# Local attention in products of one head each (64 rows by 32 columns), with the values' product placed beside the next tile's scores

## The chip, the cores and the metric

The kernel runs on one core of one Trainium2 chip. The metric is the device time of one execution in microseconds (us); lower is better. Three runs of the kernel before took 1142.04, 1142.9 and 1143.69 us, so the median is 1142.9 us.

## The reference

The program computes an attention over local windows, and two feed-forward stages behind it. All arrays are fp32.

```python
# q, k, v: (4, 8, 768, 64); mem_k, mem_v: (4, 8, 8, 64)
for c in range(nc):                       # chunks of 32 queries
    l_start, r_end = max(0, 32*c - 16), min(S, 32*c + 32 + 8)
    k_full = concat([mem_k, k[:, :, l_start:r_end]])   # up to 64 keys
    scores = scale * q_c @ k_full.T
    a = exp(scores - max); a = a / (sum(a) + 1e-9)
    out[:, :, c_start:c_end] = a @ v_full
x = out as (3072, 512)                    # heads side by side
x = (sigmoid(x @ w_gate) * (x @ w_val)) @ w_out        # 512 -> 1536 -> 512
x = silu(x @ w_in) ; x = x @ w_out2                    # 512 -> 2048 -> 512
```

## The kernel before, in words

Tokens are cut into 24 tiles of 128 (`NTILE`), and four tiles make a block of 512 (`BLOCKS1`). A tile has 4 chunks of 32 queries and 8 heads, so 32 pairs of chunk and head, each with 32 queries against 64 keys.

**Attention of one tile.** It has four parts that the program places one by one.
- Scores (`att_scores`): 16 fp32 products. Each takes two heads at once: the queries lie in a tile with zeros beside them (`qh` has 16x2x32 columns, half of them zero), so that 128 rows by 64 columns of weights hold two heads of 64 dimensions with 32 queries each. 64 keys stream through. Two such products stand side by side in TensorE's columns (`scv[cp*64 : ...]`). The profile's tile is `sc`, line L195. VectorE then takes the maximum and subtracts it (L208, L209), ScalarE takes the exponential (L210, tile `e`).
- Normalising (`att_norm`): four VectorE operations, L216 to L219.
- Turning (`att_turn`): four 128x128 transposes on TensorE (L225, tile `pt`), copied out by ScalarE (L226, tile `at`).
- Values' product (`att_pv`): 16 fp32 products with 32 columns of weights and 128 streaming columns (two heads side by side, `vb` has zeros for the other head), four side by side (L235, tile `px`); VectorE places the result in `x32` with a block transpose (L242).

**Stages.** In the opening stage the four tiles of the first block are done one after the other, with spare transposes of the identity (`idle`, tile `warm`, L389) between their parts; the queries, keys and values come by DMA from SP's queue, and the first three weights of the gated stage behind them. Then come six blocks of the gated stage. In each, `f` runs over 12 slices: a gate product `pg` and a value product `pv` (12 matmuls each, L269), their sigmoid and product on ScalarE and VectorE, and one slice late the output product `y` (12 matmuls, L89 to L93). Each slice has three steps: after `pg` (step 0), after `pv` (step 1) and after `y` (step 2). A hand-written table (`events`) puts the parts of the next block's four attention tiles at steps: scores at step 3, 11, 19 and 27 of a block's 36, normalising 2 later, turning 4 later, the values' product 6 later. Beside the first block the weights are split into high and low parts (`Feed`), beside the others the second stage's weights are prepared (`prepare2`). At the last slice of a block `split_x` makes the next block's `x` from `x32`: four ScalarE casts (L81), four VectorE subtractions (L84). After the sixth block follows the second stage (`pair2`, `out2`), which has no attention in it.

PSUM has eight banks: two `m` (`pg`, `pv`), four `y` (in the opening stage also `sc` and `px`), two `att` (`sc`, `pt`, `px` of the loop).

Of the kernel before, what the change touches and what calls it, by code (L numbers as in the profile page):

```python
# [15 lines left out]
P = 128  # L16
# [19 lines left out]
NQ = ()  # L36
# [10 lines left out]
def moe_kernel(ctx: ExitStack, tc: tile.TileContext, qh, kh, vh, wg, wv, wo, w2i, w2o, out):  # L47
# [6 lines left out]
    ps = ctx.enter_context(tc.tile_pool(name="ps", bufs=1, space=PSUM))  # L54

# [16 lines left out]
    def ps_y(name):  # L72
        return ps.tile([P, 512], F32, tag="y", name=name, bufs=4)

    def ps_a(name):
        return ps.tile([P, 512], F32, tag="att", name=name, bufs=2)
# [90 lines left out]
    def att_load_qk(t, qb, kt):  # L167
        nc.sync.dma_start(out=qb.rearrange("p g u q -> p (g u q)"), in_=qh[t])
        nc.sync.dma_start(out=kt.rearrange("p a c k -> p (a c k)"), in_=kh[t])
        q_t[t], k_t[t] = qb, kt  # L170

    def att_load_v(t, vb):
        n = 4 // len(vb) * 256
        for h, v in enumerate(vb):
            for u in range(2):
                nc.sync.dma_start(
                    out=v[u * 64 : u * 64 + 64, u].rearrange("p c j d -> p (c j d)"),
                    in_=vh[t, u * 64 : u * 64 + 64, h * n : h * n + n],
                )
        v_t[t] = vb  # L180

    def zero_v(vb, eng):
        for v in vb:
            for u in range(2):
                eng.memset(v[u * 64 : u * 64 + 64, 1 - u], 0.0)

    def att_scores(t, ps_sc, e):
        sc = ps_sc(f"sc{t}")
        scv = sc.rearrange("p (c2 a k) -> p c2 a k", c2=2, a=4)
# [12 lines left out]
        if t % TPB == 0:  # L202
            nc.vector.memset(scv[0:64, 0, :, NMEM : NMEM + LEFT], NEG)
        if t % TPB == TPB - 1:
            nc.vector.memset(scv[64:128, 1, :, WIN - RIGHT : WIN], NEG)
        s3 = sc.rearrange("p (g k) -> p g k", k=WIN)
        m = att.tile([P, 8, 1], F32, tag="m", name=f"m{t}", bufs=2)
        nc.vector.tensor_reduce(m, s3, axis=AX.X, op=ALU.max)  # L208
        nc.vector.tensor_tensor(out=e, in0=s3, in1=m.to_broadcast([P, 8, WIN]), op=ALU.subtract)  # L209
        nc.scalar.activation(out=e, in_=e, func=AF.Exp, scale=SCALE)  # L210
        e_t[t] = e

    def att_norm(t, eng=nc.vector):
        e = e_t[t]
# [4 lines left out]
        eng.tensor_tensor(out=e, in0=e, in1=r.to_broadcast([P, 8, WIN]), op=ALU.mult)  # L219

    def att_turn(t, ps_pt, at):
        e = e_t.pop(t).rearrange("p g k -> p (g k)")
        pt = ps_pt(f"pt{t}")
        for i in range(4):
            nc.tensor.transpose(pt[:, i * P : (i + 1) * P], e[:, i * P : (i + 1) * P], ident)  # L225
        nc.scalar.copy(at.rearrange("p a b q -> p (a b q)"), pt)  # L226
        at_t[t] = at

    def att_pv(t, ps_px, xt, off):
# [726 lines left out]
```

## Time and profile before

| | |
|---|---|
| median of 3 runs | 1142.9 us |
| the profiled execution | 1142.29 us |
| its span | 1140.3 us |
| TensorE (PE) busy | 1128.1 us, 99% |
| VectorE (DVE) busy | 640.3 us, 56% |
| ScalarE (ACT) busy | 486.8 us, 43% |
| granted TensorE clock | 1.00 of full speed, in all 40 slices |

PE's rows are matmuls; PEld's are their weight loads, which overlap them. A row's duration is that of one instruction from its start to its modelled end; matmuls overlap, so the distance between starts, and the pieces of the chain of waits, tell what a matmul costs in a stream. A matmul on plain fp32 is recorded as two rows: 16 products of `sc` are 32 rows. DMA queues are written as SPq.

### The profile page before, as it was taken

The numbers are of one execution on the slowest core, as the hardware profiler recorded it, in microseconds if no ns is written. First come the engines' busy times: TensorE is split into PE (matmuls) and PEld (weight loads), VectorE is DVE, ScalarE is ACT, GpSimd is POOL, SyncE is SP. The second block draws the span as 40 slices with busy tenths as digits, with TensorE's granted clock in tenths as the row PEclk, the third lists the DMA queues.
The fourth block names the chain that finished last, engine by engine and source line by source line (L and its number), as shares of the span: only waits on it lengthen the run. The fifth ranks groups of instructions, "written<-read, shape, count | busy, mean of one in ns | idle before, by whom it ended". The sixth has DMA issues, their size and how long they took to land.

```text
span 1140.3 us, 15875 instructions
## 1 busy us (share of the span) xinstructions
PE 1128.1 (99%) x6319; PEld 924.6 (81%) x6319; DVE 640.3 (56%) x947; ACT 486.8 (43%) x708; POOL 49.4 (4%) x44
## 2 busy tenths in 40 slices
PE   7999999999999999999999999999999999999998
PEld 6788888888888887888878888888888888888887
DVE  7887744555454545554454433448843479543665
ACT  2766533343344424443332324444534445344442
POOL 1000000000000000000000001101011110011000
PEclk9999999999999999999999999999999999999999
DMA  9898766667675766676573446575665566655552
GB/s 312 308 301 281 283 220 207 230 198 228 219 230 186 222 215 213 213 235 209 175 245 142 147 158 230 193 282 198 228 214 194 213 258 223 228 191 205 189 214 79
DMA packets 79209, 248.50 MB, mean 218 GB/s; under 512 B 7584, under 2 KB 23968, under 8 KB 69920
## 3 DMA queue, kind: packets, MB, share of 16 engines
q1 hardware_dynamic: 79136, 247.49, 63.7%
q8 instruction: 50, 0.82, 0.3%
q14 instruction: 23, 0.19, 0.0%
HBM read 199.23 MB, written 48.23 MB: 217 GB/s over the span
## 4 chain that ended last, share of the span: by engine, by line
PE 95%; DMA 4%; DVE 1%; SPq 0%; ACT 0%; issue 0%; DVEq 0%; ACTq 0%
PE o L786 20%; PE c L673 20%; PE pv L269 17%; PE pg L269 16%; PE y L89 6%; PE y L91 6%; PE y L93 6%; PE sc L195 2%; PE px L235 2%; DMA vA<-in_vh_dram 1%; DMA stg_wo<-in_wo_dram 1%; PE pt L225 1%; DMA stg_wg<-in_wg_dram 1%; DMA yd<-y 1%; DMA w2i_d<-coi 0%; DMA k<-in_kh_dram 0%
## 5 line engine op out<-in xcount | busy, mean ns | idle before, releaser
L673 PE MATMUL c<-xp,wr 128*128 128x512 f32 x1008 | 229.1, 389 | 0.0
L786 PE MATMUL o<-gf,wr 128*128 128x512 f32 x1008 | 229.0, 389 | 0.0
L673 PEld LDWEIGHTS c<-xp,wr 128*128 128x128 f32 x1008 | 189.2, 188 | 39.3
L786 PEld LDWEIGHTS o<-gf,wr 128*128 128x128 f32 x1008 | 189.2, 188 | 39.3
L269 PE MATMUL pg<-x,w 128*128 128x512 f32 x864 | 209.9, 392 | 2.0 <-ACT x L81 2.0
L269 PE MATMUL pv<-x,w 128*128 128x512 f32 x864 | 210.9, 393 | 0.2 <-DVE sg L284 0.2
L269 PEld LDWEIGHTS pg<-x,w 128*128 128x128 f32 x864 | 160.6, 188 | 37.1 <-ACT x L81 2.9
L269 PEld LDWEIGHTS pv<-x,w 128*128 128x128 f32 x864 | 160.2, 188 | 35.6 <-issue 2.4
L84 DVE TENSOR_TENSOR gf<-g,gf 128x1024 fp32r<-128x1024 f32 x84 | 103.8, 1239 | 49.9 <-ACT gf L81 49.6
L81 ACT CAST gf<-g 128x1024 fp32r<-128x1024 f32 x84 | 88.1, 1053 | 86.8 <-PE o L786 71.5
L286 ACT CAST g<-sg 128x512 fp32r<-128x512 f32 x72 | 44.7, 621 | 136.3 <-DVE sg L284 136.3
L279 ACT ACTIVATE sg<-pg 128x512 f32<-128x512 f32 x72 | 42.9, 596 | 93.4 <-PE pg L269 79.5
L693 POOL TENSOR_TENSOR s<-s,s 128x512 f32<-128x512 f32 x24 | 36.0, 1498 | 956.2 <-ACT s L692 956.2
L289 DVE TENSOR_TENSOR g<-sg,g 128x512 fp32r<-128x512 f32 x72 | 49.8, 691 | 42.5 <-ACT g L286 42.5
L645 DVE TENSOR_TENSOR s<-c,s 128x512 f32<-128x512 f32 x48 | 33.2, 691 | 65.1 <-PE c L673 63.1
L89 PE MATMUL y<-g,wor 128*128 128x512 f32 x240 | 66.2, 397 | 0.7 <-DVE y L547 0.7
L284 DVE TENSOR_TENSOR sg<-pv,sg 128x512 f32<-128x512 f32 x72 | 49.3, 685 | 29.6 <-PE pv L269 29.6
L91 PE MATMUL y<-g,wor 128*128 128x512 f32 x240 | 64.3, 390 | 0.0
L93 PE MATMUL y<-g,wor 128*128 128x512 f32 x240 | 64.1, 389 | 0.0
L648 DVE TENSOR_TENSOR g<-g,g 128x1024 f32<-128x1024 f32 x48 | 58.4, 1216 | 0.0
L651 ACT ACTIVATE g<-s 128x512 f32<-128x512 f32 x48 | 30.3, 632 | 54.1 <-DVE s L645 54.1
L91 PEld LDWEIGHTS y<-g,wor 128*128 128x128 f32 x240 | 45.1, 188 | 9.6
(113 smaller groups left out, 987.5 us busy)
## 6 DMA issues: line engine op xcount, KB each, us to landing
wr<-w2o_d SPq DMA_DIRECT2D x42, 1024.0 KB, 4.8
wor<-wo_d SPq DMA_DIRECT2D x60, 512.0 KB, 4.8
wr<-w2i_d SPq DMA_DIRECT2D x24, 1024.0 KB, 5.1
wr<-w2i_d SPq DMA_DIRECT2D x24, 768.0 KB, 4.4
w2o_d<-coo SPq DMA_DIRECT2D x56, 256.0 KB, 2.9
w2i_d<-coi SPq DMA_DIRECT2D x24, 512.0 KB, 3.0
qA<-in_qh_dram SPq DMA_DIRECT2D x21, 512.0 KB, 5.0
k<-in_kh_dram SPq DMA_DIRECT2D x21, 512.0 KB, 5.7
```

What stands on the lines that cost most here:

```text
L81: nc.scalar.copy(hi, src)
L84: lo_eng.tensor_tensor(out=lo, in0=src, in1=hi.bitcast(F32), op=ALU.subtract)
L89: nc.tensor.matmul(o, w_hi, x_hi, start=first, stop=False)
L91: nc.tensor.matmul(o, w_hi, x_lo, start=False, stop=False)
L93: nc.tensor.matmul(o, w_lo, x_hi, start=False, stop=last)
L269: nc.tensor.matmul(o[:, :n], w[:, pw, kt * P : (kt + 1) * P], x[kt][:, px, :n], start=i == 0, stop=i == len(steps) - 1,)
L284: nc.vector.tensor_tensor(out=sg[:, :n], in0=psv[:, :n], in1=sg[:, :n], op=ALU.mult)
L286: nc.scalar.copy(g[:, 0, :n], sg[:, :n])
L289: nc.vector.tensor_tensor(out=g[:, 1, :n], in0=sg[:, :n], in1=g[:, 0, :n].bitcast(F32), op=ALU.subtract)
L648: nc.vector.tensor_tensor(out=o, in0=a, in1=b_, op=ALU.subtract)
L673: nc.tensor.matmul(o, w[:, pw, i % 4, kt * P : (kt + 1) * P], X[i][:, px, kt], start=first and j == 0, stop=j == 5, skip_group_check=not f ...
L786: nc.tensor.matmul(c[at[i], dp], w[:, pw, pl, dp * P : (dp + 1) * P], f[:, px, pl], start=i in (A11, S1, S2) and pp == 0 and j == 0, stop= ...
```

## The change

- The data come without zeros and without doubled keys: `qh` has 512 columns instead of 1024, `kh` 768 instead of 1024 (two neighbouring chunks share one stretch of 96 keys), and the values' tile 1024 instead of 2048. The clearing of the values' tiles (`zero_v`) goes. Each tile has three loads (queries, keys, values).
- Scores: 32 products instead of 16, each of one head and chunk: 64 rows by 32 columns of weights, 64 keys streaming. Consecutive products take the eight places of a grid of two row halves (`u`) and four column quarters (`c`). The two row halves write to two PSUM banks.
- Values' product: 32 products instead of 16, on the same grid, with 64 streaming columns instead of 128.
- In the loop the values' product of a tile and the next tile's scores stand together ("meet"), in one PSUM tile of two banks, and the tiles of a block begin 9 steps apart, the first four at 3, 11, 18 and 26. Normalising comes 4 steps after the scores, turning 6 after.
- In the opening stage the multiplication of three of the four tiles goes from VectorE (one 128x512 operation) to ScalarE (eight of 128x64).
- PSUM: `att` is one tile of two banks instead of two tiles of one; in the opening stage `sc` and `px` take turns in two tiles of two banks; the second stage opens its own two banks.

On TensorE in the loop the rows below are from the first block (`px_973` and `sc_1042` are the sixth tile's values' product and the seventh tile's scores; `pg`, `pv`, `y` are the gated stage's matmuls). Before, at its place between `y` and `pg`, and between `pv` and `y`:

```order
L93 MATMUL y_3_605<-g_4_881,wo_895 128x512
L235 MATMUL px_973<-vA,at_921 32x128 x16
L269 MATMUL pg_6_1004<-x_0_445,w_928 128x512 x2
...
L269 MATMUL pv_6_1028<-x_3_454,w_928 128x512
L195 MATMUL sc_1042<-k_816,qA 64x64 x16
L89 MATMUL y_0_602<-g_5_959,wo_993 128x512
```

Now, at one of its places, between `y` and `pg`:

```order
L96 MATMUL y_2_755<-g_7_1367,wo_1381 128x512
L96 MATMUL y_3_756<-g_7_1367,wo_1381 128x512
L243 MATMUL sx_1459<-v_1215,at_1408 32x2x32 x32
L189 MATMUL sx_1459<-k_1251,q_1250 32x64 x32
L281 MATMUL pg_9_1547<-x_0_579,w_1414 128x512 x2
```

Two insertions of 16 products in the stream of large matmuls have become one of 64 smaller ones.

On VectorE at the end of the first block (`px_1462` and `sx_1709` hold the last tile of the second block; `x_0` to `x_3` are the low parts of the new `x`; `sg_11` is the gated product that frees `pv`'s bank). Before:

```order
L289 TENSOR_TENSOR g_10_1423<-sg_10_1387,g_10_1423 128x512
L242 STREAM_TRANSPOSE x_1_727<-px_1462 128x4x4x32
L130 TENSOR_TENSOR wo_1482<-t_wo_1441,wo_1482 128x512
L84 TENSOR_TENSOR x_0_1499<-x_1_727,x_0_1499 128x512
L84 TENSOR_TENSOR x_1_1502<-x_1_727,x_1_1502 128x512
L84 TENSOR_TENSOR x_2_1505<-x_1_727,x_2_1505 128x512
L84 TENSOR_TENSOR x_3_1508<-x_1_727,x_3_1508 128x512
L284 TENSOR_TENSOR sg_11_1460<-pv_11_1486,sg_11_1460 128x512
```

Now:

```order
L301 TENSOR_TENSOR g_10_1663<-sg_10_1629,g_10_1663 128x512
L252 STREAM_TRANSPOSE x_1_924<-sx_1709 128x4x128
L204 TENSOR_REDUCE m_1782<-sx_1709 128x8
L205 TENSOR_TENSOR e_1744<-sx_1709,m_1782 128x2x4x64
L133 TENSOR_TENSOR wo_1786<-t_wo_1688,wo_1786 128x512
L87 TENSOR_TENSOR x_0_1803<-x_1_924,x_0_1803 128x512
L87 TENSOR_TENSOR x_1_1806<-x_1_924,x_1_1806 128x512
L87 TENSOR_TENSOR x_2_1809<-x_1_924,x_2_1809 128x512
L87 TENSOR_TENSOR x_3_1812<-x_1_924,x_3_1812 128x512
L296 TENSOR_TENSOR sg_11_1707<-pv_11_1790,sg_11_1707 128x512
```

The maximum and the subtraction of the next tile's scores now stand between the placing of the values and the new `x`.

On ScalarE in the opening stage (`e` are the exponentials, `at` the copies of the turned tiles, `stg_wg` the first weights). Before:

```order
L210 ACTIVATE e_84<-e_84 128x512
L210 ACTIVATE e_w<-e_w 128x512 x2
L226 COPY at_260<-pt_261 128x512
L210 ACTIVATE e_w<-e_w 128x512
L226 COPY at_307<-pt_308 128x512
L226 COPY at_351<-pt_352 128x512
L107 ACTIVATE stg_wg_132<-stg_wg_132 128x512
L226 COPY at_387<-pt_388 128x512
```

Now:

```order
L211 ACTIVATE e_w<-e_w 128x512
L223 ACTIVATE e_90<-e_90,r_236 128x64 x8
L211 ACTIVATE e_w<-e_w 128x512
L231 COPY at_296<-pt_297 128x512
L223 ACTIVATE e_w<-e_w,r_310 128x64 x8
L211 ACTIVATE e_w<-e_w 128x512
L231 COPY at_366<-pt_367 128x512
L223 ACTIVATE e_w<-e_w,r_380 128x64 x8
L231 COPY at_433<-pt_434 128x512
L110 ACTIVATE stg_wg_114<-stg_wg_114 128x512
L231 COPY at_485<-pt_486 128x512
```

Three groups of eight small multiplications have come in between the exponentials and the copies.

The core of the diff:

```diff
     def att_load_v(t, vb):
-        n = 4 // len(vb) * 256
-        for h, v in enumerate(vb):
-            for u in range(2):
-                nc.sync.dma_start(
...
+        nc.sync.dma_start(out=vb, in_=vh[t])
         v_t[t] = vb
-    def att_scores(t, ps_sc, e):
...
+    def att_scores(t, sx, e):
+
+        sc = sx[:, :, :256].rearrange("p u (a k) -> p u a k", a=4)
         qb, kt = q_t.pop(t), k_t.pop(t)
-        for c2 in range(2):
-            for a in range(4):
-                for cp in range(2):
-                    c = 2 * c2 + cp
+        kv = kt.rearrange("p (a c k) -> p a c k", a=4, c=2)
+        for a in range(4):
+            for c in range(4):
+                for u in range(2):
+                    r = slice(u * 64, u * 64 + 64)
+                    g = (4 * a + c) * CH
                     nc.tensor.matmul(
-                        scv[cp * 64 : cp * 64 + 64, c2, a],
-                        qb[:, 4 * a + c].rearrange("p u q -> p (u q)"),
-                        kt[:, a, c],
+                        sc[c * CH : c * CH + CH, u, a],
+                        qb[r, g : g + CH],
+                        kv[r, a, c // 2, c % 2 * CH : c % 2 * CH + WIN],
                         start=True,
                         stop=True,
                     )
...
     def att_norm(t, eng=nc.vector):
...
+        if eng is nc.scalar:
+            for g in range(8):
+                nc.scalar.activation(out=e[:, g], in_=e[:, g], func=AF.Copy, scale=r[:, g])
+        else:
+            eng.tensor_tensor(out=e, in0=e, in1=r.to_broadcast([P, 8, WIN]), op=ALU.mult)
...
+    def att_pv(t, px, xt, off):
+
         at, vb = at_t.pop(t), v_t.pop(t)
-        px = ps_px(f"px{t}")
         for c in range(4):
-            for j in range(4):
-                q0 = 64 * (c % 2) + 32 * (j % 2)
-                nc.tensor.matmul(
-                    px[32 * j : 32 * j + 32, c * P : (c + 1) * P],
-                    at[:, c // 2, j // 2, q0 : q0 + 32],
-                    vb[c * len(vb) // 4][:, :, c % (4 // len(vb)), j],
...
+            for a in range(4):
+                for u in range(2):
+                    r = slice(u * 64, u * 64 + 64)
+                    g = a * P + c * CH
+                    o = px[a * CH : a * CH + CH, u].rearrange("p (h x) -> p h x", h=2)
+                    nc.tensor.matmul(
+                        o[:, :, c * CH : c * CH + CH],
+                        at[r, g : g + CH],
+                        vb[r, (4 * c + a) * D : (4 * c + a + 1) * D],
...
+        for t in range(n0, NTILE + 1):
+            at = 9 * (t - n0) - 3 if t >= 2 * n0 else (3, 11, 18, 26)[t - n0]
+            events.setdefault(at, []).append(("meet", t))
+            if t < NTILE:
+                events.setdefault(at + 4, []).append(("norm", t))
+                events.setdefault(at + 6, []).append(("turn", t))
...
+                if what == "meet":
+                    sx = ps_att(f"sx{t}")
+                    steps = []
+                    if t > n0:
...
+                        steps.append(att_pv(t - 1, sx[:, :, 256:], x32[bn], jj * P))
+                        prefetch_v(t)
+                    if t < NTILE:
+                        steps.append(att_scores(t, sx, e_tile(t)))
+                        prefetch(t + 1)
+                    for step in steps:
+                        step()
```

The functions' last lines (the softmax in `soften`, the placing in `place`) are now handed back and run after both products have been issued.

## Rows read from the trace of the kernel before

**Rows 1.** The page: busy us of each engine (share of the span) x instructions.
```profile
PE 1128.1 (99%) x6319; PEld 924.6 (81%) x6319; DVE 640.3 (56%) x947; ACT 486.8 (43%) x708; POOL 49.4 (4%) x44
```

**Rows 2.** By stage: busy PE, PEld, DVE, ACT, POOL; PE clock, DMA share, GB/s.
```profile
0.00:29.10 29.10, 22.04 (x351) 19.16 (x351) 21.32 (x41) 8.49 (x14) 4.81 (x14) 1.00 0.93 315
29.10:150.00 120.90, 120.68 (x775) 97.25 (x776) 96.49 (x173) 76.72 (x125) 0.00 (x0) 1.00 0.84 288
150.00:571.90 421.90, 421.52 (x2707) 342.11 (x2709) 209.76 (x387) 166.75 (x253) 0.00 (x0) 1.00 0.65 212
```

**Rows 3.** Chain of waits in order of time, first block: start, duration, what.
```profile
128.02 2.72 PE pg L269 x12
130.74 1.01 PE px L235 x32
131.75 2.94 PE pv L269 x12
...
145.58 2.72 PE pg L269 x12
148.29 1.08 PE sc L195 x32
149.38 2.95 PE pv L269 x12
```

**Rows 4.** TensorE's timeline at 191.1 and 197.8 us, each once short, once whole.
```profile
191.10 0.32 PE L235 MATMUL px<-vA,at 128*32 128x128 f32 x4
...
191.10 1.08 PE L235 MATMUL px<-vA,at 128*32 128x128 f32 x32
...
197.77 0.28 PE L195 MATMUL sc<-k,qA 128*64 128x64 f32 x2
...
197.77 1.15 PE L195 MATMUL sc<-k,qA 128*64 128x64 f32 x32
```

**Rows 5.** Tiles sc and px: durations in ns (least/median/most), first and last start.
```profile
L195 PE MATMUL sc<-k,qA x672: 222/222/270, 5.7 to 554.0; 128*64 128x64 f32 x168
...
L235 PE MATMUL px<-vA,at x672: 272/273/297, 17.9 to 572.0; 128*32 128x128 f32 x168
```

**Rows 6.** Timeline of the opening stage: start, us, what [idle before, releaser].
```profile
1.37 4.14 PE L389 MATMUL warm<-ident 128*128 128x128 f32 x22 [1.37 <-POOL ident masks.py:199]
...
5.69 1.15 PE L195 MATMUL sc<-k,qA 128*64 128x64 f32 x32 [0.18 <-DMA k<-in_kh_dram]
...
23.62 0.69 ACT L107 ACTIVATE stg_wg<-stg_wg 128x512 f32<-128x512 f32 x1 [2.62 <-DMA stg_wg<-in_wg_dram]
...
24.20 0.58 ACT L226 COPY at<-pt 128x512 f32<-128x512 f32 x1
...
29.10 3.22 PE L269 MATMUL pg<-x,w 128*128 128x512 f32 x12 [2.02 <-ACT x L81]
```

**Rows 7.** Groups of the opening stage: busy us, mean ns, idle before.
```profile
L226 ACT COPY at<-pt 128x512 f32<-128x512 f32 x4 | 2.3, 575 | 1.9 <-PE pt L225 1.9
L209 DVE TENSOR_TENSOR e_w<-sc,m 128x512 f32<-128x512 f32 x3 | 2.1, 692 | 0.1
L219 DVE TENSOR_TENSOR e_w<-e_w,r 128x512 f32<-128x512 f32 x3 | 2.1, 691 | 0.1
L216 DVE TENSOR_REDUCE r<-e_w 128x8 f32<-128x512 f32 x3 | 2.0, 665 | 0.0
...
L210 ACT ACTIVATE e_w<-e_w 128x512 f32<-128x512 f32 x3 | 1.9, 631 | 6.5 <-DVE e_w L209 6.5
```

**Rows 8.** Timeline at 235.8 to 247.2 us, the end of a block.
```profile
235.76 0.41 ACT L81 CAST coi<-fi 128x256 fp32r<-128x256 f32 x1
...
240.65 1.08 PE L235 MATMUL px<-vA,at 128*32 128x128 f32 x32
...
245.94 0.68 DVE L284 TENSOR_TENSOR sg<-pv,sg 128x512 f32<-128x512 f32 x1
...
247.23 2.88 PE L269 MATMUL pg<-x,w 128*128 128x512 f32 x12
```

More of the change, by code (lines that the diff above doesn't have):

```diff
@@ L35 @@
 LV = 1
-NQ = ()
 NJ = 8
@@ L201, in att_scores, with soften @@
                     )
[L202 to L210, printed above, removed]
-        e_t[t] = e
+        e_t[t] = e
+        def soften():
+            if t % TPB == 0:
+                nc.vector.memset(sc[0:CH, :, :, 0:LEFT], NEG)
+            if t % TPB == TPB - 1:
+                nc.vector.memset(sc[3 * CH : 4 * CH, :, :, WIN - RIGHT : WIN], NEG)
+            m = att.tile([P, 2, 4, 1], F32, tag="m", name=f"m{t}", bufs=2)
+            nc.vector.tensor_reduce(m, sc, axis=AX.X, op=ALU.max)
+            nc.vector.tensor_tensor(
+                out=e.rearrange("p (a u k) -> p u a k", a=4, u=2),
+                in0=sc,
+                in1=m.to_broadcast([P, 2, 4, WIN]),
+                op=ALU.subtract,
+            )
+            nc.scalar.activation(out=e, in_=e, func=AF.Exp, scale=SCALE)
+        return soften
     def att_norm(t, eng=nc.vector):
-        e = e_t[t]
+        e = e_t[t].rearrange("p (g k) -> p g k", g=8)
         r = att.tile([P, 8, 1], F32, tag="r", name=f"r{t}", bufs=2)
@@ L227, in att_turn, with place @@
+    def att_turn(t, pt, at):
+        e = e_t.pop(t)
+        for a in range(4):
+            nc.tensor.transpose(pt[:, a * P : (a + 1) * P], e[:, a * P : (a + 1) * P], ident)
+        nc.scalar.copy(at, pt)
         at_t[t] = at
-    def att_pv(t, ps_px, xt, off):
+    def att_pv(t, px, xt, off):
         at, vb = at_t.pop(t), v_t.pop(t)
-        px = ps_px(f"px{t}")
         for c in range(4):
-            for j in range(4):
-                q0 = 64 * (c % 2) + 32 * (j % 2)
-                nc.tensor.matmul(
-                    px[32 * j : 32 * j + 32, c * P : (c + 1) * P],
-                    at[:, c // 2, j // 2, q0 : q0 + 32],
-                    vb[c * len(vb) // 4][:, :, c % (4 // len(vb)), j],
-                    start=True,
-                    stop=True,
-                )
-        nc.vector.transpose(
-            out=xt[:, :, off : off + P].rearrange("p k (c q) -> p c k q", c=4),
-            in_=px.rearrange("p (c k q) -> p c k q", c=4, k=4),
-        )
+            for a in range(4):
+                for u in range(2):
[6 more added lines that the diff above has]
+                        vb[r, (4 * c + a) * D : (4 * c + a + 1) * D],
+                        start=True,
+                        stop=True,
+                    )
+        def place():
+            nc.vector.transpose(
+                out=xt[:, :, off : off + P].rearrange("p (u h) x -> p u h x", u=2),
+                in_=px.rearrange("p u (h x) -> p u h x", h=2),
+            )
+        return place
@@ L315, in at_tile, with v_tile @@
+        def v_tile(t):
+            return att.tile([P, 16 * D], F32, tag="v", name=f"v{t}", bufs=1)
         def at_tile(t):
-            return att.tile([P, 2, 2, P], F32, tag="at", name=f"at{t}", bufs=1)
+            return att.tile([P, 512], F32, tag="at", name=f"at{t}", bufs=1)
         def e_tile(t):
-            return att.tile([P, 8, WIN], F32, tag="e", name=f"e{t}", bufs=1)
+            return att.tile([P, 512], F32, tag="e", name=f"e{t}", bufs=1)
         def flat(i, name):
             w = w_slot(i, name).bitcast(F32)
-            return [w[:, h].rearrange("p a b -> p (a b)") for h in range(2)]
@@ L340, in moe_kernel @@
-        for t in range(n0):
-            if t == 0:
-                make_identity(nc, ident)
-            zero_v(vs[t], nc.gpsimd if t % 2 else nc.vector)
+            kv = flat(4 + t, f"kv{t}")
+            vs.append(kv[:, :1024])
+            ks.append(kv[:, 1024 : 1024 + 8 * (WIN + CH)])
+            qs.append(qq[:, (t - 1) * 512 : t * 512])
+            es.append(eq[:, (t - 1) * 512 : t * 512])
+        make_identity(nc, ident)
         wo_d = dram.tile([NF1, P, 2, 512], F32, tag="wo_d", name="wo_d")
```

136 lines of the change are left out of this document (58 added, 78 removed).

## The prediction, made before the changed kernel ran

> **What bounds the kernel now.** I read the page first: TensorE is busy 1128.1 of 1140.3 us, the other engines at most 56% [rows 1]. An average can hide stages, so the table by stage came next. The opening stage, up to the first gated matmul at 29.10 us, is the only one in which TensorE has gaps: 22.04 of 29.10 us busy, with the DMA engines at 0.93. In the first block it is busy 120.68 of 120.90 us, in the other five 421.52 of 421.90 [rows 2]. So from 29.1 us on every microsecond of TensorE's time that the attention takes stands in the result, and waits on other engines cost nothing there now. Third, the chain of waits gives the price of attention in that stream: twelve large matmuls take 2.72 us, a scores piece 1.08 and the twelve behind it 2.95, so scores cost 1.08 + 0.23 = 1.31 us; a values piece costs 1.01 + 0.22 = 1.23 us [rows 3]. Together 2.54 us a tile, 50.8 us for the loop's 20 tiles. Last, I opened the timeline around one of each, to see what these pieces are made of.
>
> **What a small product costs.** Thirty-two rows of scores, of 0.222 us each, fill 1.15 us: their starts are spread over 0.93 us. Two stand side by side, and the second starts about 7 ns behind the first (0.28 us for two, 0.270 for the longest one) [rows 4, 5]. So there are 16 pairs in 15 steps of (0.93 - 0.007)/15 = 0.0615 us. The values' 32 rows, 0.272 us each, are spread over 1.08 - 0.27 = 0.81 us; four start within 0.32 - 0.297 = 0.023 us, which makes 8 groups in 7 steps of (0.81 - 0.02)/7 = 0.113 us [rows 4, 5]. The step follows the streaming columns (64 against 128) and not how many products stand side by side: two and four run at the same speed each. Taking 16 x 0.0615 from 1.31 and 8 x 0.113 from 1.23 leaves 0.33 us in both cases: the frame of one insertion, which is the change into small products and back.
>
> **The loop after the change.** A tile now has 32 scores products and 32 values' products, 64 rows each, all with 64 streaming columns. Eight side by side make 8 + 8 groups. If the step stays at 0.0615 us, these take 0.98 us. Eight starts need 7 x 0.007 = 0.05 us, which fits inside a step; at the end the spread adds 0.03 to the frame, 0.36 us, paid once instead of twice. A meeting then costs 1.34 us against 2.54. There are 19 whole meetings, one with scores alone and one with values alone (0.49 + 0.36 = 0.85 us each): 19 x 1.34 + 2 x 0.85 = 27.2 us against 50.8. The gain is 23.5 us. In general, with s for the average distance between small rows, the loop changes by 2560 s - 43.2 us (2560 rows, 21 frames of 0.36, less 50.8). That s is the unknown: no row of before has eight side by side, or products in two row halves. The near end is 0.0615/8 = 7.7 ns. The far end is the distance the values' rows keep today, 0.113/4 = 28.3 ns, which would add 29.2 us. Below the near end lies only the 7 ns of neighbouring starts, 1.8 us better still. I take 7.7 ns, because the step was the same for two and for four, and the starts of neighbours are close enough for eight.
>
> Here a rule of the Trainium skill speaks against the change. The rows give 7 ns between neighbours of one group, yet on average no row follows another by less than 28.3 ns [rows 4]. Its page "TensorE: Matmul & The Clock Gate", section "Wait — 56ns, not 53.3ns?", says that the distance from matmul to matmul never falls under about 25 ns however few columns stream. Read as an average over the whole engine this gives 2560 x 0.025 - 43.2 = 21 us more in the loop, an estimate from that page, and about 1161 us in all. Part 3 of the same page, on packing small matmuls, gives about 4 ns for each further place of the grid; the 7 ns agree with this one, so I read the 25 ns as a bound for one place.
>
> **The rest of the loop.** The transposes, the softmax operations and their durations stay. At the end of a block, VectorE has maximum and subtraction (689 and 692 ns by today's scores, so 1.4 us) between the placing of the values and the new x, and ScalarE has the exponential, 0.63 us, ahead of the casts [rows 7]. In the block end that I looked at, values start at 240.65, the product that frees the value bank starts at 245.94, the new block's gate at 247.23 and its value product 2.72 us later, at 249.95 [rows 3, 8]. Freed at 246.6 now, the bank comes 3.3 us early; about 2.1 us of added work leaves 1.2. The new x is nearer: its last low part ends when L284 starts, 1.3 us before the gate, though only the first of the four is needed at once and the others 0.68 us apart each. I price the four block ends that carry scores at 0.2 us each, 0.8 in all, between 0 and 4 x 2.1 = 8.4. In the first block VectorE is at 96.49 of 120.90 us [rows 2]; losing some 6 us of TensorE's time there raises this to 84%, still no bound. DMAs only get smaller, and SP waits for fewer of them.
>
> **The opening stage.** Before, the last copy of a turned tile (24.20) sits behind the first weights' operation, which waited for its DMA until 23.62; from that copy to the first gate at 29.10 pass 4.9 us [rows 6]. The first eight loads shrink from 8 x 512 KB to 4 x (256 + 384) KB, 1.6 MB less, at 315 GB/s 5.0 us [rows 2]: those weights would land near 18.6 us, and they are no longer last. The engines' own chain is. The first scores can't start before the 22 spare transposes end at 5.51, and before they started at 5.69 [rows 6]: nearly nothing is gained there. VectorE loses three multiplications of 691 ns, and ScalarE gets three groups of eight [rows 7]. One of these eight has 64 columns; a cast of 256 columns takes 0.41 us [rows 8], an operation of 512 takes 0.63 [rows 7], so by a straight line 0.25 us, 2.0 for eight (between 0.63, as one operation, and 8 x 0.41 = 3.3). ScalarE then needs 2.0 + 0.63 + 0.58 = 3.2 us a tile. The first group starts when two tiles have been through maximum and subtraction (1.4 us each) and one through its row sum and what follows it (1.1), so near 5.5 + 0.7 + 2.8 + 1.1 = 10.1 us; three times 3.2 ends the third tile near 19.7; the fourth is normalised on VectorE beside it and turned, and its copy starts some 1.1 us later, near 20.8. With the same 4.9 us behind it the first gate comes at 25.7, 3.4 us earlier. The ends: 5.0 earlier (bytes alone), and 0.5 later (3 x 1.3 us more for the eights).
>
> **The sum**, against the profiled execution's own 1142.29 us (0.6 under the median of 1142.9): 1142.3 - 23.5 - 3.4 + 0.8 = 1116.2. I predict 1116 us.
>
> **Rivals.**
> - *Only four places run at once* (0.12): the two row halves take turns, as if the columns' quarters alone counted. For it: no row before uses half of the rows. Against: nothing in the rows ties a start to its neighbour. s = 0.0615/4 = 15.4 ns, the loop changes by -3.8 us, the opening by about -3: 1142.3 - 6.8 + 0.8 = 1136 us. The change would then not do what it says; only the smaller frame pays.
> - *The supply of small rows is the limit* (0.13), and the kernel gets slower: twice as many rows and weight loads come in an unbroken run of 128 rows, four times as long as any today. For it: no stretch of the trace has rows closer than 28.3 ns on average. Against: that distance is explained by the streaming columns to a few ns, in both shapes. At 28.3 ns the loop is 29.2 us longer and the opening still some 2 us shorter: about 1170 us. The change turns into a loss where 2560 s - 43.2 - 3.4 + 0.8 passes zero, at s = 17.9 ns.
> - *The products are as fast as forecast, but waits take the place of what was saved* (0.07): the block ends at their full price (7.6 us more than I count), or the opening's longer gaps, near 3 us against 2.02 today, lower TensorE's clock to the 1.2 GHz level for the first gate and value products, 24 x 0.227 = 5.4 us. The rows show 1.00 throughout [rows 2], so I give this little. One alone gives 1122 or 1124 us, both 1129.
>
> **How the numbers follow.** The forecast has 0.68, with 1110 to 1124 as its own range: the near bound of s and a full 5.0 in the opening on one side, block ends at half price on the other. The range that should hold 8 in 10 goes on from there to the half-speed rival and a little over it: 1108 to 1140. It leaves out the supply rival and some of the rest. A change of 0.2%, 2.3 us, is about what a measurement of this kernel can tell from none. Faster by more takes in the forecast, the first rival and most of the third: 0.85. Slower by more is the supply rival, 0.12 of its 0.13; the same 0.03.
>
> **What would show each step.** In the timeline of a meeting: 64 rows of values and 64 of scores, the last start about 1.0 us behind the first; eight starts within 0.06 us, then a pause. If the starts come evenly every 15 or 25 ns, one of the first two rivals holds. In the chain: one piece of scores and values together of some 1.1 us, the twelve matmuls behind it 0.2 longer than 2.72. TensorE's idle time after the first gate stays under 2 us in total, otherwise the third rival has its part. The first gate starts between 24 and 27 us, and eight small multiplications take near 2.0 us. The prediction is wrong if a meeting costs more than 1.8 us in the chain, or if the gates at block ends wait for x.

## The result and the profile after

The changed kernel takes 1126.57 us (median of 4 runs, 1125.71 to 1127.12) against 1142.88 us beside it: a ratio of 0.9857, 95% interval 0.984 to 0.9874. It is 16.3 us faster. The forecast was 26 us faster: the sign and the wide range held, the likeliest case's own range (1110 to 1124) did not. Two terms of the sum were mis-sized: the distance of small products in a long piece, and the opening stage, in which TensorE ran out of instructions.

The page's line of busy times, and that of the queue that brings TensorE's instructions (packets, MB, share of the DMA engines). Before, the queue had moved 50 packets, 0.82 MB, for 12,638 matmuls and weight loads; now it is 62 for 15,710, some 253 a packet both times:

```profile
PE 1112.1 (99%) x7855; PEld 917.8 (82%) x7855; DVE 635.0 (56%) x938; ACT 490.8 (44%) x732; POOL 45.3 (4%) x36
...
q8 instruction: 62, 1.02, 0.4%
```

The same three stages as in [rows 2], with the same columns:

```profile
0.00:29.10 29.10, 21.85 (x607) 18.85 (x607) 15.51 (x31) 13.73 (x36) 0.70 (x6) 0.94 0.79 295
29.10:150.00 120.90, 120.06 (x1073) 98.21 (x1074) 99.20 (x179) 78.95 (x128) 0.00 (x0) 0.99 0.76 269
150.00:571.90 421.90, 421.90 (x3760) 347.39 (x3760) 215.69 (x395) 170.26 (x262) 0.00 (x0) 1.00 0.61 205
```

From 150 to 571.9 us TensorE has no gap at all, and the list of its waits has none at the block end before that: the block ends cost nothing. The opening stage has the same busy time in far more instructions, less DMA, and a granted clock of 0.94 where it was 1.00.

The chain of waits through a meeting, and through scores alone (start, us, what; counts are a little low where records are missing), beside [rows 3]:

```profile
40.20 0.79 PE sx L189 x53
40.99 2.99 PE pv L281 x12
...
63.48 0.79 PE sx L243 x53
64.27 0.65 PE sx L189 x42
64.92 2.94 PE pg L281 x12
```

A meeting costs 0.79 + 0.65 + (2.94 - 2.72) = 1.66 us, against 2.54 before and 1.34 forecast; scores alone cost 0.79 + 0.27 = 1.06. TensorE's timeline of the same meeting, its first part cut out once (start, us, what):

```profile
63.42 0.45 PE L243 MATMUL sx<-v,at 64*32 64x64 f32 x32
...
63.42 0.86 PE L243 MATMUL sx<-v,at 64*32 64x64 f32 x64
64.08 0.85 PE L189 MATMUL sx<-k,q 64*32 64x64 f32 x64
64.85 3.01 PE L281 MATMUL pg<-x,w 128*128 128x512 f32 x12
```

One row lasts 0.216 us. The first 32 rows start within 0.45 - 0.216, some 0.24 us, 7.7 ns apart: the eight places do work together, at the forecast distance. But 64 rows start within 0.64 us and all 128 within 64.08 + 0.85 - 0.22 - 63.42 = 1.29 us. The 96 rows behind the first 32 are (1.29 - 0.24)/96 = 11 ns apart; over the whole meeting it is 10.2.

The opening stage, answering to [rows 6] (TensorE, then ScalarE, then TensorE):

```profile
5.30 0.86 PE L189 MATMUL sc<-k,q 64*32 64x64 f32 x64
...
9.29 0.79 PE L189 MATMUL sc<-kv,q_w 64*32 64x64 f32 x57
13.64 0.31 PE L189 MATMUL sc<-kv,q_w 64*32 64x64 f32 x7 [3.56 <-issue]
...
11.03 2.02 ACT L223 ACTIVATE e<-e,r 128x64 f32<-128x64 f32 x8 [0.47 <-DVE r L220]
...
24.89 0.59 ACT L231 COPY at<-pt 128x512 f32<-128x512 f32 x1 [0.26 <-PE pt L230]
...
29.94 4.48 PE L281 MATMUL pg<-x,w 128*128 128x512 f32 x12 [1.96 <-ACT x L84]
```

After 57 of the 64 rows of the third scores tile TensorE stands for 3.56 us, in the middle of one tile's products, and the profile names no releaser. The last copy comes at 24.89 us, not at the forecast 20.8, and the first gate at 29.94, 0.84 us later than before. Its twelve matmuls then take 4.48 us where they took 3.22. Not all of them are slow: the first seven start 234 to 335 ns apart as before, and from about the eighth on, into the value product behind them, the distance is 427 ns, which is the 1.2 GHz level. By stretches (columns as in [rows 2], granted clock third from the end) the clock fell twice: once behind the 3.56 us of idle time, and once 1.6 us into the first gate:

```profile
14.60:17.80 3.20, 3.20 (x46) 2.87 (x45) 1.76 (x5) 2.34 (x8) 0.00 (x0) 0.50 1.04 416
31.60:34.90 3.30, 3.30 (x9) 2.62 (x9) 3.09 (x7) 1.96 (x4) 0.00 (x0) 0.50 0.16 31
```

What the second fall cost is the time from the first gate to the second one, before and after:

```profile
34.90 2.99 PE L269 MATMUL pg<-x,w 128*128 128x512 f32 x12
...
37.32 0.39 PE L281 MATMUL pg<-x,w 128*128 128x512 f32 x1
```

That is 34.90 - 29.10 = 5.80 us and 37.32 - 29.94 = 7.38 us, 1.58 us more.

### The profile page after: what moved, and what is told of

It is laid out like the page before. It is cut to its first block, busy times and chain, and to the rows that moved or that the text cites. A ratio compares the mean times of both kernels' runs of the same rounds, so it can differ in the third digit from the quotient of the medians.

```text
span 1125.3 us, 18936 instructions
## 1 busy us (share of the span) xinstructions
PE 1112.1 (99%) x7855; PEld 917.8 (82%) x7855; DVE 635.0 (56%) x938; ACT 490.8 (44%) x732; POOL 45.3 (4%) x36
## 4 chain that ended last, share of the span: by engine, by line
PE 96%; DMA 2%; DVE 0%; SPq 0%; ACT 0%; issue 0%; DVEq 0%
PE o L808 20%; PE c L695 20%; PE pv L281 18%; PE pg L281 17%; PE y L94 6%; PE y L92 6%; PE y L96 6%; PE sx L243 1%; PE sx L189 1%; DMA k<-in_kh_dram 1%; PE pt L230 1%; DMA kv<-in_vh_dram 1%; DMA yd<-y 1%; SPq L172 0%; SPq L171 0%; DVE x L252 0%
```

## Experiments on the loop

The theory: TensorE's instructions are fed at a limited pace. The first 32 rows of a piece stand ready and run at the forecast 7.7 ns; what follows is fed more slowly. The rival: the eight places themselves are full.

**Half of the columns** (m1). The kept half of the keys and of the values' columns is computed in the loop, the rest set to zero.

```
-   kv[r, a, c // 2, c % 2 * CH : c % 2 * CH + WIN]
+   kv[r, a, c // 2, c % 2 * CH : c % 2 * CH + 32]       # same in values: 32 of 64 columns
+   nc.vector.memset(sc[:, :, :, 32:], 0.0)              # and the other half of the values
```

> The changed kernel with half of the streaming columns left out in the loop: each small product has 32 columns instead of 64 (half of the keys, half of the values' columns; the halves that are left out are set to zero by VectorE). Theory, supply: after its first 32 rows a meeting is fed at 16.7 ns a product (8.3 ns a row) and has pauses of its own; a product half as long changes nothing in that: meetings keep 1.2 to 1.3 us between first and last start, and the time stays within 4 us of the changed kernel's 1126.6 (1122 to 1127). Rival, the eight places are full: with half the columns the distance halves, a meeting's starts spread over some 0.7 us, and the loop is 11 to 13 us shorter: 1114 to 1116.

1126.65 us (ratio 0.9859, 0.9844 to 0.9874). TensorE's timeline of a meeting, its first 32 rows cut out once:

```profile
61.48 0.35 PE L245 MATMUL sx<-v,at 64*32 64x32 f32 x32
...
61.48 0.76 PE L245 MATMUL sx<-v,at 64*32 64x32 f32 x64
62.09 0.75 PE L189 MATMUL sx<-k,q 64*32 64x32 f32 x64
62.77 2.56 PE L286 MATMUL pg<-x,w 128*128 128x512 f32 x10
```

From the first row to the next large matmul pass 1.29 us, against 1.43 in the changed kernel: half of the streaming saves a tenth. Of the values' 64 rows the first 32 start within 0.16 us instead of 0.24, while the 32 behind them take 0.40 us in both kernels. So behind the first 32 rows the eight places are not what is full; something that does not depend on the streaming columns is, and I call it the feed. This run leaves the number and the size of the weight loads as they were, so it does not tell instructions that come slowly from weight loads that go slowly. Against the second stands that 33 weight loads start within 0.20 us at the head of a piece; a run that separates the two was not made. The total did not even fall by 20 x 0.14 = 2.8 us, though the first gate runs at the 2.4 GHz level here (3.19 us): VectorE has the memsets in addition, TensorE waits 1.7 us once for VectorE's product of a gate and a value, and some 2 us stay unexplained.

**Half by half** (m2). The order of the loops alone.

```
-   for a in range(4): for c in range(4): for u in range(2):
+   for u in range(2): for a in range(4): for c in range(4):
```

> The changed kernel with another order of the same products: all of one row half (heads 0 to 63 of the partitions) before all of the other, in scores and in values, so that neighbours in the order use four places and not eight. Theory, TensorE takes instructions in order with at most some 32 rows queued: only four places work at a time, a row each 61.5/4 = 15.4 ns, a meeting of 128 rows costs 2.0 + 0.2 us instead of 1.66, and the loop is some 10 us longer: 1135 to 1139. Rival, supply alone sets the distance of 10 ns, whatever the places: the time stays at 1126 to 1128.

1132.27 us (ratio 0.9903, 0.9887 to 0.992), 5.7 more than the changed kernel, between the two expectations. The timeline of a meeting, its first 0.27 us cut out, and the chain of another:

```profile
63.50 0.47 PE L243 MATMUL sx<-v,at 64*32 64x64 f32 x18
...
63.50 0.99 PE L243 MATMUL sx<-v,at 64*32 64x64 f32 x64
64.30 0.98 PE L189 MATMUL sx<-k,q 64*32 64x64 f32 x64
```

```profile
109.26 0.92 PE sx L243 x61
110.19 0.79 PE sx L189 x60
110.97 2.99 PE pg L281 x12
```

In the 0.27 us in which the changed kernel starts 32 rows, 18 start here, 15 ns apart as four places allow. Rows 33 to 64 of a piece then take 0.40 us, as in the changed kernel, so the loss is smaller than I expected: 1.98 us a meeting against 1.66, about 6 us over the loop. Eight places in turn in the order of the program are worth that much; this part of the forecast's mechanism is shown.

**Apart** (m3). Scores one step ahead of the values instead of behind them in one piece.

```
-   events.setdefault(at, []).append(("meet", t))
+   events.setdefault(at - 1, []).append(("scores", t))
+   events.setdefault(at, []).append(("values", t))
```

> The changed kernel with scores and values at separate places in the loop, one step of some 3 us apart, instead of in one piece: the new products without the meeting. By the chain of the changed kernel scores alone cost 0.79 + 0.27 = 1.06 us and a meeting 1.66. Theory, a frame of 0.36 to 0.4 us is paid once for each insertion, and rows cost 10.2 ns in a piece of 64 as in one of 128: 2.12 us a tile, 19 x 0.46 = 8.7 us more, 1134 to 1137. Rival, the long unbroken run of 128 rows is what makes rows dear (10.2 ns where the first 32 take 8.3): pieces of 64 come cheaper, 1.5 to 1.8 us for the two, and the time is at 1124 to 1130.

1135.55 us (ratio 0.994, 0.9923 to 0.9957). The chain:

```profile
156.34 0.79 PE sx L189 x53
157.13 2.94 PE pg L281 x12
160.07 0.79 PE sx L243 x53
160.86 2.94 PE pv L281 x12
```

Twice 0.79 + 0.22 = 2.02 us against 1.66: the meeting saves one frame of 0.36 us, 19 x 0.36 = 6.8 us. The other 2 of the 9.0 us are waits that this order adds (scores for the copy of a turned tile 1.3 us, values for VectorE 0.6).

**Bursts of 32 rows** (m4): m3, with the scores in two pieces one step apart.

```
+   events.setdefault(at - 2, []).append(("scores0", t))     # a = 0, 1
    events.setdefault(at - 1, []).append(("scores", t))      # a = 2, 3
```

> The kernel of m3 with the scores of a tile split once more, into two pieces of 32 rows, one step of the loop apart. Theory, the first 32 rows of every piece stand ready and run at 8.3 ns (267 ns), and only what follows is fed at the slower pace: a piece of 32 costs 0.27 + 0.4 = 0.67 us, two 1.34 against 1.06 for one of 64, 20 x 0.28 = 5.6 us more than m3: 1140 to 1143. Rival, every small row costs 10.2 ns wherever it stands: a piece of 32 costs 0.33 + 0.42 = 0.75 us, 20 x 0.44 = 8.8 us more than m3: 1143 to 1146; the starts of a piece would be spread over 0.32 us and not 0.26.

1144.91 us (ratio 1.0023, 1.0013 to 1.0033): slower than the kernel before. The chain around the two pieces:

```profile
159.00 0.38 PE sx L188 x32
159.38 1.12 PE y L92 x4
160.51 0.92 PE y L94 x4
161.43 0.91 PE y L96 x4
162.33 0.39 PE sx L206 x32
162.72 2.95 PE pg L298 x12
```

Thirty-two rows start within 0.24 us (7.7 ns each) in every one of these pieces, so a piece costs 0.38 + 0.21 = 0.59 or 0.39 + 0.23 = 0.62 us, cheaper than the theory's 0.67. The two cost 1.21 us against 1.01 for one of 64. Two pieces stand apart in 17 of the 20 tiles (in the other three no large matmul lies between them): 17 x 0.20 = 3.4 us. The rest of the 9.4 us over m3 is not the price of rows: TensorE waits 4.9 us for ScalarE's copy of the turned tile instead of 1.3, and it has one more stretch at the 1.2 GHz level, from 61.4 to 64.8 us, which costs some 1.7 us. By the total the rival seemed right, by its pieces the theory is. Frames eat what the faster rows give.

## Experiments on the opening stage

The theory: at 13.6 us TensorE had used up its instructions. The trace shows them coming in packets of 16,384 bytes; one such packet starts at 11.35 us and lasts 0.99 us, in a stretch in which the DMA engines are full of loads, and none has come before it in the span. The rival: a hidden wait on data.

**More spare transposes** (o2).

```
-   idle(22)
+   idle(30)
```

> The changed kernel with 30 spare transposes ahead of the first scores instead of 22: 8 more transposes, 16 more rows (8 weight loads, 8 matmuls). Instruction refill: the stall comes 16 rows earlier in the stream, after 49 rows of the third scores tile instead of 57, and lasts about as long or a little less, as the refill lands at the same time, near 13.6 us. Rival, a hidden wait on data: it stays after 57 rows, or goes, as the scores come 0.9 us later.

TensorE's timeline of o2 (start, us, what [idle before, releaser]; so in the fences below):

```profile
10.09 0.72 PE L189 MATMUL sc<-kv,q_w 64*32 64x64 f32 x49
13.34 0.34 PE L189 MATMUL sc<-kv,q_w 64*32 64x64 f32 x15 [2.52 <-issue]
```

The stall moved from 57 rows to 49: by exactly the 8 matmuls (and 8 weight loads) that were put ahead. A wait on data would have stayed at its row. So the place is set by the count of instructions. The run took 1126.61 us.

The other runs bear this out. Counted with TensorE's semaphore instructions, all its idle times of over 0.3 us without a releaser in the opening stage, in all the traces of the change and of its variants, come after 449, 705, 961 or 1217 instructions of the trace. These are 256 apart, one packet if an instruction has 64 bytes. In matmuls that is after 221, 347, 474 or 601. The third of these places in o2 and in o8, which is described below (busy times and counts from the start to just before TensorE goes on; its matmuls come first):

```profile
0.00:24.00 24.00, 18.45 (x474) 16.09 (x475) 10.95 (x23) 11.75 (x33) 0.70 (x6) 1.00 0.90 335
...
0.00:23.80 23.80, 20.16 (x474) 10.58 (x474) 12.53 (x26) 12.35 (x34) 0.70 (x6) 1.00 0.74 273
```

And where TensorE had to wait without a releaser, it went on 2.2 to 2.8 us after the start of a packet, whenever that was.

**Fewer instructions for the same spare work** (o1).

```
-   for _ in range(n): nc.tensor.transpose(warm[:, :P], ident, ident)
+   nc.tensor.matmul(o, ident, ident.unsqueeze(1).to_broadcast([P, w // P, P]), ...)   # w up to 512
```

> The changed kernel with the spare products of the opening stage in fewer instructions: one matmul of up to 512 columns where eight transposes stood, the same length in time. Theory, instruction refill: in the changed kernel TensorE stands 3.56 us after 57 of 64 rows of the third scores tile, with nothing that the profile shows behind it, because the instructions that were fetched ahead (two pieces of 16 KB) are used up and the third piece sits behind the loads. Some 52 fewer rows are issued up to there now, so the third tile should end without a stall near 10.2 us (13.95 now), TensorE should keep its 2.4 GHz level, and the first gate should start at 25.5 to 27.5 us (29.94 now): 1121 to 1124 us. Rival, a wait on data that the records don't show: the stall stays at the 57th row of that tile, and the time at 1126 to 1127.

TensorE's timeline of o1, from the third scores tile to the first gate:

```profile
10.16 0.86 PE L189 MATMUL sc<-kv,q_w 64*32 64x64 f32 x64
...
22.68 0.77 PE L243 MATMUL px<-kv,at 64*32 64x64 f32 x54
24.94 1.00 PE L243 MATMUL px<-kv,at 64*32 64x64 f32 x74 [1.49 <-issue]
...
29.09 4.66 PE L281 MATMUL pg<-x,w 128*128 128x512 f32 x12 [2.10 <-ACT x L84]
```

The third scores tile now runs through, as expected. But the time is 1126.94 us (0.9859, 0.9844 to 0.9874): no gain. A later refill stops TensorE instead, in the values (1.49 us, and 0.78 us before), the gate is only 0.85 us earlier, and its matmuls are still slow. One stall was taken away and the next in the row took its place.

**The multiplications back on VectorE** (o4: o1 with that edit undone).

```
-   att_norm(i - 1, nc.scalar if i < n0 else nc.vector)
+   att_norm(i - 1, nc.vector)
```

> The kernel of o1 (spare products in few instructions) with the opening stage's first three multiplications by the reciprocal sum put back on VectorE: one operation of 0.69 us each instead of eight on ScalarE that take 2.02 us. In o1 the chain goes through one such group of eight (11.76 to 13.78 us), and later through two idle times of TensorE with nothing behind them in the records (0.78 us at 19.57, 1.49 us at 23.45). Theory, the refills of instructions pace the rest of the stage (in o1 pieces of 16 KB start at 11.88, 17.83, 22.49 and 27.05 us): what is saved on ScalarE is lost at the next refill, the first gate stays at 28 to 29.5 us, the time at 1125 to 1127. Rival, ScalarE's eights set the end of the stage: the first gate starts 1.3 to 3 us earlier, at 26 to 27.8 us, and the time is 1123.5 to 1125.5.

1127.22 us (0.9865, 0.9848 to 0.9882), the first gate at 28.94 us, with 1.66 us of idle time in the same values piece. Where the multiplications stand makes no difference that these runs can tell, as long as the refills pace the stage.

**Fewer loads** (o5). Value tiles and first weights are filled with a constant, not loaded.

```
-   nc.sync.dma_start(out=vb, in_=vh[t])
+   nc.gpsimd.memset(vb, 0.01)          # t < 4; the first four weight units likewise
```

> The changed kernel with most of the loads of its opening stage left out: the four value tiles and the first four weight units are filled with a constant by GpSimd instead of loaded (so the first block's values and gates are not those of the reference); about 4 MB of 6.6 MB less on the DMA engines before the first gate. Theory, the refill of TensorE's instructions waits behind the loads on the DMA engines: its packet, asked for when the first 256 instructions are used up, near 7.6 us, starts well before the 11.35 us of the changed kernel, at 8.5 to 10 us, and the idle time after the 57th row of the third scores tile shrinks from 3.56 us to under 1.8. Rival, the refill takes its 3.7 us by itself whatever else is moved: start near 11.3 us, idle time 3 to 3.6 us.

TensorE's timeline of o5 in the third scores tile:

```profile
9.71 0.79 PE L195 MATMUL sc<-kv,q_w 64*32 64x64 f32 x57
12.57 0.31 PE L195 MATMUL sc<-kv,q_w 64*32 64x64 f32 x7 [2.06 <-issue]
```

The one run took 1124.09 us. The stall is at the same row and shorter, 2.06 us; the first packet starts at 10.30 us. Both fall short of what I expected; the keys and queries are still being loaded then. This first stall alone shows little: in five traces with one and the same opening stage (the changed kernel, a_again, m1, m3, m4) it lasts 2.45 to 3.56 us, and the first packet starts at 10.67 to 11.35. The second packet is clearer: it starts at 13.67 us, 1.1 us after TensorE goes on at 12.57. In the changed kernel it starts at 17.73, 4.1 us after 13.64, and at 17.58 to 18.12 in the other four.

**Two weight units loaded late** (o6: o1, 1 MB issued near 19 us instead of at the start).

```
-   feed1.load(4)                # ahead of the first scores
+   feed1.load(2)
    ...
    prefetch_v(n0)
+   feed1.load(4)
```

> The kernel of o1 (spare products in few instructions), and the loads of the third and fourth weight units, 1 MB that is needed from 30 us on, are issued behind the value load of the loop's first tile, near 19 us, instead of with the first loads. Theory, refills wait behind the loads that are queued on the DMA engines (with 4 MB of them left out, the second refill of the stage started 1.1 us after the stall's end, against 4.1 us in the changed kernel): the engines run dry near 18.5 us instead of 21.8, so the third and fourth refill come 1 to 3 us sooner, the idle time of 1.49 us that o1 has at 23.45 goes, and the first gate starts at 26.8 to 28.2 us (29.09 in o1): 1123.5 to 1126 us. Rival, the refill's delay doesn't come from the queued loads, or what they move is needed earlier than I read: the gate stays at 29 us or later, the time at 1126 to 1129.

TensorE's timeline of o6, the third and fourth values piece and the gate:

```profile
27.25 1.36 PE L243 MATMUL px<-kv,at 64*32 64x64 f32 x74 [3.40 <-issue]
...
31.53 3.21 PE L281 MATMUL pg<-x,w 128*128 128x512 f32 x12 [0.92 <-ACT x L84]
```

The opposite of the gain that I expected, from the same cause: the late loads stood in the queues just when the third refill was asked for. It starts at 24.85 us (22.49 in o1), and the idle time grows to 3.40 us. Still the time is 1127.05 us (0.9856, 0.9841 to 0.987): the gate is 1.4 us later than in the changed kernel run beside it (30.10), but its twelve matmuls run at the 2.4 GHz level, 3.21 us. The stretch at 1.2 GHz lies ahead of the gate here, from 27.1 to 30.5 us, behind the 3.40 us of idle time.

**The same, with VectorE's multiplications** (o7: o4 and the edit of o6).

> The kernel of o4 (spare products in few instructions, the opening multiplications on VectorE) with the same two loads issued late, as in o6. Theory, with the refills out of the way the engines' own chain counts, and by this chain one multiplication of 0.69 us beats eight of 2.02 us together: the first gate at 26.5 to 27.8 us, at or up to 1 us ahead of o6; 1123 to 1126 us. Rival, VectorE is then the crowded engine of the stage (in o4 the chain runs through it from 9.7 to 20.0 us): the gate is as late as in o6 or later, 1124 to 1127.

1129.18 us (0.9871, 0.9857 to 0.9886), the gate at 31.97 us, with 3.85 us of idle time at the same place. Of the rival only the late gate held, and not its reason: the refill, not one of the two engines, sets the stage. The gate explains 0.4 of the 2.1 us over o6. The rest lies in the last block of the profiled execution: TensorE waits 2.2 us for y there instead of 0.7, and has a stretch at the 1.2 GHz level from 580.7 to 584.1 us that o6 has not.

**The changed kernel again** (a_again, beside o6 and o7).

> The changed kernel as it is, once more, for a comparison with o6 and o7 on the same chip: 1125.7 to 1127.5 us, the first gate near 29.9 us and an idle time of 2.5 to 3.6 us inside the third scores tile, after 57 rows.

1126.99 us (0.9857, 0.984 to 0.9873); 2.97 us of idle time after the 57th row, the gate at 30.10.

**Late units behind the refill** (o8: o1, with the two units issued behind the last copy, the loop's first values later still).

```
    att_turn(i - 2, ...)                      # ScalarE's copy
+   if i == n0 + 1:
+       for u in units[2:4]: u.load(nc.scalar)
```

> The kernel of o1, with the loads of the third and fourth weight units and of the loop's first values moved further back than in o6: the two units are issued on ScalarE's queue behind the last copy of a turned tile (near 23 us), the values behind the first step of the weight feed. In o6 those 1.5 MB were issued near 19 us, when the third refill was being asked for, and that refill started at 24.85 us instead of o1's 22.49: the idle time inside the third values piece grew from 1.49 to 3.40 us. Theory, refills wait behind what is queued on the DMA engines: with nothing queued from 18.5 to 23 us the third refill starts by 20.5 us, the idle time in the values goes, the first gate starts at 27.2 to 28.2 us with TensorE at the 2.4 GHz level (twelve matmuls in 3.2 us instead of 4.4), and the time is 1122.5 to 1125 us. Rival, the third refill comes near 22.5 us all the same: idle time of about 1.5 us, gate at 29 us, 1126 to 1127.5 us. A miss of both would be the units landing too late for their casts near 30 us, with TensorE waiting for them behind the first gate.

TensorE's timeline of o8 at the same places:

```profile
23.86 1.00 PE L243 MATMUL px<-kv,at 64*32 64x64 f32 x74 [0.66 <-issue]
...
28.02 4.71 PE L281 MATMUL pg<-x,w 128*128 128x512 f32 x12 [2.10 <-ACT x L84]
```

The third refill starts at 21.39 us, the idle time there falls to 0.66 us and the gate comes at 28.02 us, 1.9 us earlier than in the changed kernel. In o6 the DMA engines are full of loads until about 24.6 us, in o1 until 22.4, in o8 they are all but empty from 20.5 us on. This refill starts at 24.85, 22.49 and 21.39 us, which is 4.1, 2.1 and 1.3 us after TensorE passed the place of the stall before it, and the idle time follows with 3.40, 1.49 and 0.66: that refills wait behind queued loads is shown by this row of three. The row also shows what is left with hardly a load in the way: 1.3 us to the packet and 2.5 from there on make 3.8, and TensorE was through with its 256 instructions in 3.1. But the time is 1126.05 us (0.9852, 0.9835 to 0.9868), not told apart from the changed kernel: the gate came as the theory said, the time did not. The gate's matmuls run at the 1.2 GHz level, as they do in the changed kernel, so the gain that I expected from the clock is missing; and 1.0 us of the 1.9 is taken back by a longer wait for y early in the last block, near 577 us. TensorE's waits of o8 from 28 us on (us in total, times, longest); the first of them is 1.3 us in the changed kernel:

```profile
PE y L92 <- DVE y L577: 2.3, 1, 2.3
PE pg L281 <- ACT x L84: 2.1, 1, 2.1
```

## Why the forecast was right in sign and wrong in size

| Step | Forecast, us | Measured, us |
|---|---|---|
| a meeting | 1.34 | 1.66 |
| loop | -23.5 | 19 x 1.66 + 2 x 1.06 - 50.8 = -17.1 |
| first gate | -3.4 | +0.84 |
| clock in the first gate and value product | 0 | 7.38 - 5.80 = +1.58 |
| block ends | +0.8 | 0 |
| waits in the loop before, for VectorE (0.4 and 0.2), that are gone | 0 | -0.6 |
| wait for y early in the last block | 0 | 1.3 - 0.7 = +0.6 |
| sum, profiled execution | 1116.2 | 1142.3 - 14.7 = 1127.6; it took 1127.06 |

From the first gate to the first gate of the last block the time fell from 548.6 to 532.1 us, by 16.5; the terms of the table for that stretch give 17.1 - 1.6 + 0.6 = 16.1.

- **The distance of small rows** failed: "the step was the same for two and for four, and the starts of neighbours are close enough for eight". For eight places at once this is right (7.7 ns in every piece of 32 rows, and 15 ns when the order allows only four). But all pieces of before had 32 rows, and I carried their step over to 128. Over a whole meeting s is 10.2 ns, and the formula of the prediction gives 2560 x 0.0102 - 43.2 = -17.1 us by it. The rival of the supply was the right mechanism at a small part of its price: 6.4 us of the 52.7 that lay between it and the forecast. m1 shows that behind the first 32 rows of a piece the columns no longer count; which part of the feed sets the pace was not taken apart, and stays open. The 25 ns that the prediction weighed as an average over the whole engine did not come true; its 7 ns between neighbours are nearer to the 4 ns that it set beside them than to 25, but they do not agree with it.
- **The frame** held: 1.66 - 1.29 = 0.37 us for a meeting, 0.36 forecast, and m3 shows that it is paid once.
- **The opening** failed in the step "the engines' own chain is" what comes last. ScalarE's eights took 2.02 us (2.0 forecast), and from the last copy to the gate passed 5.05 us (4.9). But the third scores tile ended at 13.95 us instead of near 10.1, for want of instructions, and the copy came at 24.89 instead of 20.8. I counted what the added instructions cost TensorE and not what it costs to bring them. In the kernel before, the first packet started at 12.91 us with 283 rows executed, TensorE reached the 449th at 18.4 us, and nothing waited for the packet: its waits gave no sign, only the place of the packets did.
- **The weights** were no longer last, as forecast: the first weights' operation on ScalarE starts at 23.95 us, right behind a copy.
- **The clock** was given little chance in the third rival; it took 1.58 of the 5.4 us named there, in some eight matmuls of the 24.
- **The block ends** cost nothing, within the bounds given (0 to 8.4). Of the signs that the prediction named, the meeting under 1.8 us, the idle time under 2 us after the first gate (1.3), the twelve matmuls longer by 0.22 us and the eights at 2.0 us are there; the groups of eight are, but only in the first 32 rows of a piece. The last start 1.0 us behind the first (1.29), the piece of 1.1 us in the chain (1.44) and the gate at 24 to 27 us are not.
- **The stages** of [rows 2] have other names in the prediction than they should: the second block begins at 137.25 us, so the row up to 150 us holds its start too, and the row up to 571.9 us ends with the fifth block. The last block has no attention in it. The sum does not rest on this.

On the refills the Trainium skill, page "Runtime: NRT & Kernel Launch", section "Instruction fetch mechanics", says that instructions come in blocks of 16 KiB (256 instructions), that the next is fetched while the current one runs, and that crossing into the next is mostly hidden. The packets agree in size, and the stalls in their distance of 256. That the crossing is hidden holds here from the first gate on; in the opening stage one crossing cost 3.56 us.

## What to carry to other kernels

A step measured in short runs of small matmuls holds for runs of that length: before a change makes them longer, ask what else may set the pace, not only how fast the array takes them. Count the instructions that a change adds ahead of the first large matmuls and look where the instruction queue's packets fall; here, beside queued loads, a refill started 4 us late. A stall with no releaser in the middle of equal instructions that moves with their count was a refill here, and taking one away showed the next.

## What the runs showed that I had not expected

- A refill of TensorE's instructions started 1.1 us after TensorE had gone on with the last of the former ones when few loads were queued, and 4.1 us after it when they were many.
- Rows of 64 x 32 with 64 columns start 7.7 ns apart for the first 32 of a piece and about 11 ns apart behind them; with 32 columns the whole piece is only a tenth shorter.
- Whether the first gate runs at 1.2 or 2.4 GHz does not follow from the idle time ahead of it alone. With 0.92 us of it (o6, o7) the twelve matmuls took 3.2 us; with 1.8 to 2.1 us (the changed kernel, o1, o8) 4.5 to 4.7. But before, 2.02 us of it went with 3.22 us [rows 6], and in o5 1.57 us with 3.20; and with 0.77 and 1.03 us (m4, m2) they took 4.7. What decides it stays open. So does why the wait for y near 577 us varies (0.5 to 2.3 us between these runs): in the changed kernel the chain goes through a store of y that takes 6.57 us there.
